# Cosine attention and a highway layer on one core: the gate's bias moved to VectorE, the norm of k moved into the exponential

## The chip, the core and the metric

The kernel runs on one core of a Trainium2 chip. A time is the device time of one execution in microseconds; the median of the runs shown counts. The core's engines work side by side and each takes its own instructions strictly in the order of the program: TensorE (PE; its weight loads are shown apart as PEld), VectorE (DVE), ScalarE (ACT), GpSimd (POOL) and SyncE (SP), which here only starts transfers. An instruction that waits holds up everything behind it on its engine.

## What is computed

```python
def _attn_ref(q, k, v, tau):                    # (8, 12, 448, 64): batch, heads, rows, depth
    q_n = q / (np.linalg.norm(q, axis=-1, keepdims=True) + 1e-06)
    k_n = k / (np.linalg.norm(k, axis=-1, keepdims=True) + 1e-06)
    scores = np.matmul(q_n, k_n.transpose(0, 1, 3, 2)) / tau
    scores = scores - np.max(scores, axis=-1, keepdims=True)
    attn = np.exp(scores)
    attn = attn / (np.sum(attn, axis=-1, keepdims=True) + 1e-09)
    return np.matmul(attn, v).astype(np.float32)

def _moe_ref(x, w_h, w_t, b_t):                 # x is (3584, 768), the weights (768, 768)
    H = np.maximum(x @ w_h, 0.0)
    T = 1.0 / (1.0 + np.exp(-(x @ w_t + b_t)))
    return (T * H + (1.0 - T) * x).astype(np.float32)
```

The attention's 12 heads of 64 columns side by side are the 768 columns of x. The scores are cosines over tau = 0.1, so they are bounded and the kernels leave the row maximum out. T is the gate and b_t its bias.

## The kernel before

The work goes by batch (8 of them), and in a batch by pairs of heads (6), 48 steps s in all. Of the 448 rows, 384 lie as three chunks on 128 partitions each (qr, kr, vr); the last 64 of two heads share the partitions of one more tile (qt, kt, vt).

For each batch the squares of q and k are summed (sq, f, n) and turned into 1/norm in rs: by a logarithm and an exponential on ScalarE for batch 0, by seven Newton steps on VectorE for the others (`steps`, lines 447 to 472). `scaled` (525) multiplies q and k of a pair by it into qn, on GpSimd or VectorE; `ktnorm` and `qtnorm` do the same for the last rows into kb. qn is then turned (queries and keys on the free side) into qT: by TensorE, with a copy out of PSUM, for batches 0 to 3, by a transposing transfer on SP for the others.

`scores` (621) is the heart. For each of three chunks of 128 keys TensorE writes the scores of both heads of a pair, 128 keys by 2 x 448 queries, into one of three pairs of PSUM banks (S, named pS), and ScalarE takes the exponential of all 896 columns in one instruction (line 643) into E, with the factor 1/tau as a constant. The last 64 keys of both heads go through a bank of the other ring of two (B, named pB) and one exponential of 512 columns (656) into Et. `attend` then multiplies E with v; a column of ones in vp gives the row sum, whose reciprocal (713) scales the result into x (715).

`ffn` (731) makes the highway layer for a batch in four groups of rows, three of 128 x 768 and one of 128 x 384. The gate's products with wt and those with wh each fill one of the three S slots; the gate's sum begins with two products of a tile of ones with the bias (bth, lines 777 and 793), which put the bias into PSUM. ScalarE takes the tanh out of PSUM (816, 817) into tt, VectorE forms max(H, 0) - x out of PSUM (830), maps tt to the gate (835), multiplies (838), and VectorE or GpSimd adds x (844) into os, from which SP stores. os is a ring of four buffers.

The order of all of this is written out by hand: `ORDER` lists the numbered operations, `SLOTS` the buffer that each takes from its ring, `MOVED` those that go to their second choice of engine. Operations of VectorE and GpSimd that are marked `port` also keep the order of the list between them. The highway layer of a batch is spread over the attention of the next. The few lines that matter are these:

```python
def fe(c=c):                                                             # line 642
    return nc.scalar.activation(R("E", s)[:, c, :, 0:448], R("S", 3 * s + c)[:, :, 0:448], AF.Exp, scale=inv_tau)
...
lt, rh = (ones[ln, 0:128], bth[ln, cols]) if cc < 0 else (xT[ln, cc, :], w_[ln, cc, cols])
```

Of the kernel before, what the change touches and what calls it, by code (L numbers as in the profile page):

```python
# [12 lines left out]
ALU = mybir.AluOpType  # L13
# [83 lines left out]
1121010122010000100121121000010222112011102100120012100102110110211012100011012310120002210110001102010110220100  # L97
1010020122111020211001100201010111200101200000000102111210001210022102001201002011102110110020112011112001020220
0001102102110100110021102212100210001220001010200122110012110211101013200000021102101220110002122102101102100010
20121001001011100201321000122201012223  # L100
""".replace("\n", "")
)

# [862 lines left out]
```

## Time and profile before

| | |
|---|---|
| median of 3 runs | 272.5 us (270.1, 272.5, 274.83) |
| span of the profiled execution, first to last instruction | 268.0 us |
| mean granted clock of TensorE | 0.967 |
| moved by the transfer engines | 43.14 MB, mean 161 GB/s |

The profile covers one execution from its first to its last instruction. The time of a run is taken outside and holds a little more than the span; the profiled execution's own time isn't listed apart, so its span stands beside the runs: 4.5 us under their median, 2.1 us under the lowest. A row that groups instructions gives line, engine, operation, output and inputs, shape and count, then the group's busy time and the mean duration of one in ns, then how long the engine had been idle before them and what ended it. A row of the timeline gives start, duration from the first start to the last end, and the same names. A row by stretches gives its bounds, its length, the busy time of the engines named in the text with the number of instructions, then TensorE's granted clock, the share of the transfer engines and GB/s.

### The profile page before, as it was taken

To read this page: it belongs to the slowest core of one execution; us is meant where nothing else is said; L and a number is where in the kernel's file an instruction comes from. 1 tells how busy PE (TensorE), PEld (TensorE's weight loads), DVE (VectorE), ACT (ScalarE), POOL (GpSimd) and SP (SyncE) were. 2 spreads that over 40 slices of the span, in tenths; PEclk is the share of its full clock that TensorE was granted. 3 is DMA by queue.
4 is the path that set the end of the run, shared out by engine and by line. 5 is a ranking of instruction groups with operands and counts; after the bars stand their busy time and mean duration, and the time that the engine had idled before them with its cause. 6 is when DMAs were issued, how large, how long until landed. Compare 5 with 4: busy or idle time off the path is not lost.

```text
span 268.0 us, 9080 instructions
## 1 busy us (share of the span) xinstructions
PE 243.8 (91%) x3783; PEld 164.3 (61%) x3783; DVE 220.0 (82%) x501; ACT 206.1 (77%) x279; POOL 116.2 (43%) x150
## 2 busy tenths in 40 slices
PE   6088987899999999999999998999999999999990
PEld 2043665667776667666766775766567757777650
DVE  6598999999999989997999988999877953556483
ACT  3378999789999989989788898969778897671210
POOL 8757359455554567335551535226132501141200
PEclk9567999999999999999999999999999999999996
DMA  7999999999969696999889999999757837123143
GB/s 131 210 192 183 178 199 210 196 183 193 149 97 224 145 172 65 192 213 199 206 136 155 186 244 162 193 137 224 173 115 214 134 63 177 59 92 120 32 181 101
DMA packets 103738, 43.14 MB, mean 161 GB/s; under 512 B 97552, under 2 KB 100624, under 8 KB 103696
## 3 DMA queue, kind: packets, MB, share of 16 engines
q0 software_dynamic: 38464, 16.32, 49.1%
q1 hardware_dynamic: 64000, 25.80, 47.4%
q8 instruction: 30, 0.49, 0.7%
q10 hardware_dynamic: 1232, 0.43, 0.7%
q14 instruction: 12, 0.10, 0.1%
HBM read 37.82 MB, written 11.01 MB: 182 GB/s over the span
## 4 chain that ended last, share of the span: by engine, by line
PE 64%; DVE 17%; DMA 8%; issue 4%; ACT 2%; POOL 2%; SPq 1%; DVEq 0%; POOLq 0%; ACTq 0%
PE pS L793 27%; PE pS L637 8%; PE pB L689 7%; PE pS L777 6%; DMA qT<-qn 6%; PE pB L652 4%; PE pB L705 3%; PE pB L685 3%; PE pB L577 3%; DMA qr<-in_q_dram 2%; DVE os L844 2%; DVE x L715 2%; DVE f L416 2%; PE pB L306 1%; DVE kb L254 1%
## 5 line engine op out<-in xcount | busy, mean ns | idle before, releaser
L643 ACT ACTIVATE E<-pS 128x896 f16<-128x896 f32 x144 | 127.4, 924 | 23.1 <-PE pS L637 21.9
L793 PEld LDWEIGHTS <-xT 64*128 64x128 f16 x1152 | 54.5, 94 | 31.2 <-issue 1.3
L793 PE MATMUL pS<-wh,xT 64*128 64x384 f16 x576 | 58.0, 323 | 0.0
L793 PE MATMUL pS<-wt,xT 64*128 64x384 f16 x576 | 57.1, 323 | 0.0
L637 PE MATMUL pS<-qT 64*128 64x384 f16 x288 | 43.5, 331 | 1.8 <-DMA qT<-qn 1.0
L689 PE MATMUL pB<-vp,E 128*128 128x65 f16 x864 | 43.3, 194 | 0.0
L830 DVE SCALAR_TENSOR_TENSOR hm<-pS,x 128x768 f16<-128x768 f32 (+1 forms) x33 | 27.3, 834 | 17.5 <-PE pS L793 6.9
L689 PEld LDWEIGHTS <-E 128*128 128x128 f16 x864 | 38.5, 98 | 0.7 <-issue 0.6
L637 PEld LDWEIGHTS <-qT 64*128 64x128 f16 x576 | 22.7, 95 | 19.5 <-issue 4.6
L254 POOL TENSOR_TENSOR qn<-kr,rs 128x384 f16<-128x384 f16 x24 | 19.8, 828 | 32.5 <-issue 10.0
L685 PE MATMUL pB<-vp,Et 128*128 128x130 f16 x144 | 31.9, 222 | 0.5 <-DVE vp L257 0.4
L844 POOL TENSOR_TENSOR os<-x,hm 128x768 f32<-128x768 f16 (+1 forms) x11 | 16.7, 1516 | 34.6 <-DVE hm L838 16.4
L817 ACT ACTIVATE tt<-pS 128x768 f16<-128x768 f32 x24 | 19.6, 821 | 14.4 <-PE pS L793 14.3
L715 DVE SCALAR_TENSOR_TENSOR x<-pB,rd 128x448 f16<-128x448 f32 x48 | 29.8, 622 | 1.1
L656 ACT ACTIVATE Et<-pB 128x512 f16<-128x512 f32 x48 | 29.1, 610 | 1.7 <-PE pB L652 1.5
L637 PE MATMUL pS<-tT,qT 64*128 64x64 f16 x282 | 27.6, 190 | 0.0
L705 PE MATMUL pB<-vp,E 128*128 128x65 f16 x288 | 18.4, 194 | 0.6 <-DVE x L715 0.6
L254 POOL TENSOR_TENSOR qn<-qr,rs 128x384 f16<-128x384 f16 x17 | 14.4, 853 | 9.0 <-DVE os L844 3.5
L844 DVE TENSOR_TENSOR os<-x,hm 128x768 f32<-128x768 f16 (+1 forms) x21 | 17.6, 836 | 0.2
L685 PEld LDWEIGHTS <-Et 128*128 128x128 f16 x144 | 14.0, 97 | 5.6 <-issue 4.1
L254 DVE TENSOR_TENSOR qn<-qr,rs 128x384 f16<-128x384 f16 x30 | 16.8, 566 | 0.5 <-POOL qn L254 0.4
L713 DVE RECIPROCAL rd<-pB 128x7 f32<-128x7 f32 x48 | 9.4, 199 | 8.4 <-PE pB L705 4.0
(110 smaller groups left out, 437.4 us busy)
## 6 DMA issues: line engine op xcount, KB each, us to landing
out_dram<-os SPq DMA_DIRECT2D x24, 384.0 KB, 3.2
vr<-in_v_dram POOLq DMA_DIRECT2D x8, 576.0 KB, 11.7
kr<-in_k_dram POOLq DMA_DIRECT2D x7, 576.0 KB, 9.9
qr<-in_q_dram POOLq DMA_DIRECT2D x7, 576.0 KB, 10.2
qt<-in_q_dram SPq DMA_DIRECT2D x16, 96.0 KB, 5.2
vt<-in_v_dram SPq DMA_DIRECT2D x16, 96.0 KB, 5.2
out_dram<-os SPq DMA_DIRECT2D x16, 96.0 KB, 2.3
kt<-in_k_dram SPq DMA_DIRECT2D x14, 96.0 KB, 6.0
```

The lines of the kernel that those rows point to most:

```text
L254: return (nc.vector if eng == "DVE" else nc.gpsimd).tensor_mul(out_, a, c)
L637: ins = nc.tensor.matmul(dst, lhsT=qT[ln, 384 + 128 * c : 512 + 128 * c], rhs=rhs, start=True, stop=True)
L643: return nc.scalar.activation(R("E", s)[:, c, :, 0:448], R("S", 3 * s + c)[:, :, 0:448], AF.Exp, scale=inv_tau)
L656: op("ACT", f"expt {s}", lambda: nc.scalar.activation(R("Et", s)[:, 64:576], R("B", ("S", s))[:, :], AF.Exp, scale=inv_tau), key + 3, r=[( ...
L685: nc.tensor.matmul(U[:, 2 * c : 2 * c + 2, :].rearrange("p g e -> p (g e)"), lhsT=Et[:, 128 + 128 * c : 256 + 128 * c], rhs=vp[:, 6:8, :]. ...
L689: ins = nc.tensor.matmul(U[:, 2 * c + ab, :], lhsT=EF[:, j, 576 * ab + 128 * c : 576 * ab + 128 * c + 128], rhs=vp[:, 3 * ab + j, :], star ...
L705: ins = nc.tensor.matmul(U[:, 6, :], lhsT=lt, rhs=rh, start=(n == 0), stop=(n == 7))
L715: op("DVE", f"ev {s}", lambda: nc.vector.scalar_tensor_tensor(out=R("x", b)[:, :, D * p : D * p + D], in0=U_()[:, :, 0:D], scalar=0.0, in1 ...
L793: ins = nc.tensor.matmul(P[:, h, 0:MH], lhsT=lt, rhs=rh, start=(part == 0 and cc == (-1 if wi == 0 else 0)), stop=(part == 1 and cc == CC ...
L817: return nc.scalar.activation(T.rearrange("p (h m) -> p h m", h=2), P[:, :, 0:MH], AF.Tanh, scale=0.5)
L830: return nc.vector.scalar_tensor_tensor(out=o_, in0=i0, scalar=0.0, in1=xs, op0=ALU.max, op1=ALU.subtract)
L844: op(en, f"out{wd} {g}", lambda: eng.tensor_add(R("os", g)[:, 0:W], xall(), R("hm", g)[:, 0:W]), at + 0.1, r=[("gg", g), ("x", b)], w=[("o ...
```

## The change

Six edits, and with them the whole order is new.

- The gate's bias is no longer put into PSUM by products. It is spread over all partitions by its load (bth, and bt2 for the narrow group), and VectorE adds it while it reads the gate's products out of PSUM, into a buffer of os (called z here); the tanh reads z instead of PSUM. This holds for all batches (`ADDED`).
- k is no longer scaled: `carried` copies it into qn, on VectorE, GpSimd or ScalarE, and `ktnorm` copies too. Its 1/norm is applied in the exponential, as a scale that is read for each partition (a key) from rs. The two heads of a pair have different norms, so the exponential of 896 columns becomes two of 448; that of the last keys stays one. tau is taken into rs. This holds for all pairs (`RAW`) but the first. rs has four buffers instead of three.
- Each weight comes in two loads instead of one, and the first products wait for the half that they use.
- More operations may go to either of two or three engines (`ENGINES` in place of `MOVED`).
- The first pair of q and k is loaded into a buffer of os.
- A second load of ScalarE's function table is written out (before, one stood ahead of the first tanh).

```diff
+    RAW = tuple(range(8))
+    ADDED = tuple(range(8))
...
-    NR = dict(..., rs=3, qn=2,
+    NR = dict(..., rs=4, qn=2,
...
-        for w_src, w_dst, nm in ((moe_w_t, wt, "wt"), (moe_w_h, wh, "wh")):
-            op("POOL", f"ld {nm}", lambda w_src=w_src, w_dst=w_dst: nc.gpsimd.dma_start(
-                w_dst[:, :, :], w_src.rearrange("(cc p) m -> p cc m", p=128)), key, w=[(nm, 0)])
-        for n in range(2):
-            op("POOL", f"ld b {n}", lambda n=n: nc.gpsimd.dma_start(bth[64 * n : 64 * n + 1, :], moe_b_t), key,
-               w=[("bth", 0)], r=[("zb", 0)])
+        op("POOL", "ld b", lambda: nc.gpsimd.dma_start(bth[:, :], moe_b_t.partition_broadcast(128)), key, w=[("bth", 0)])
...
+        for hf in range(2):
+            for w_src, w_dst, nm in ((moe_w_t, wt, "wt"), (moe_w_h, wh, "wh")):
+                op("POOL", f"ldw {nm} {hf}", lambda w_src=w_src, w_dst=w_dst, hf=hf: nc.gpsimd.dma_start(
+                    w_dst[:, 3 * hf : 3 * hf + 3, :], w_src.rearrange("(cc p) m -> p cc m", p=128)[:, 3 * hf : 3 * hf + 3]), key,
+                   w=[(nm, hf)])
...
+    def carried(t, b, p, key):
+        s = 6 * b + p
+        eng = pick("DVE", "POOL", "ACT")
+        op(eng, f"kc {s}", lambda: copied(
+            eng, R("qn", s // 2)[:, s % 2, t].rearrange("l c ab d -> l ab c d"),
+            rows(t, b, p, p + 1)[:, :, 0, :].rearrange("l ab (c d) -> l ab c d", c=NCH)), key,
+           r=[rowtok(t, b, p)], w=[("qn", s // 2, s % 2)], port=True)
...
             def fe(c=c):
+                if raw(b, p):
+                    at = col(b, p) + 6 + c
+                    for ab in range(2):
+                        ins = nc.scalar.activation(R("E", s)[:, c, ab, 0:448], R("S", 3 * s + c)[:, ab, 0:448], AF.Exp,
+                                                   scale=R("rs", b)[:, 0, at + NCH * ab : at + NCH * ab + 1])
+                    return ins
                 return nc.scalar.activation(R("E", s)[:, c, :, 0:448], R("S", 3 * s + c)[:, :, 0:448], AF.Exp, scale=inv_tau)
...
-            R("Et", s)[:, 64:576], R("B", ("S", s))[:, :], AF.Exp, scale=inv_tau), key + 3,
+            R("Et", s)[:, 64:576], R("B", ("S", s))[:, :], AF.Exp,
+            scale=R("rs", b)[:, 0, 6 + p : 7 + p] if raw(b, p) else inv_tau), key + 3,
...
-                for cc in range(lo - (1 if wi == 0 and lo == part == 0 else 0), hi):
+                for cc in range(lo - (1 if biased and lo == part == 0 else 0), hi):
...
+                if added:
+                    def biased_gate():
+                        P, Z = R(*bank_of(g, 0, tail)), R("os", ("z", g))
+                        if tail:
+                            return nc.vector.tensor_add(Z[:, 0:MH], P[:, 0, 0:MH], bt2[:, :])
+                        return nc.vector.tensor_add(Z.rearrange("p (h m) -> p h m", h=2), P[:, :, 0:MH],
+                                                    bth.rearrange("p (h m) -> p h m", h=2))
+
+                    op("DVE", f"bz{1 if tail else 2} {g}", biased_gate, at, r=[("Pd", g, 0), ("bt2" if tail else "bth", 0)],
+                       w=[("z", g)], u=[bank, ("os", ("z", g))])
+
...
+                    if added:
+                        return nc.scalar.activation(T[:, 0:W], R("os", ("z", g))[:, 0:W], AF.Tanh, scale=0.5)
```

Of the new tables, two lines stand for all:

```diff
-18 17 2 3 5 0 77 20 19 33 82 21 6 23 11 4 83 24 29 22 76 1 16 8 73 86 28 74 41 25 36 80 40 9 42 27 26 35 32 43
+18 20 24 28 5 29 11 30 0 21 19 22 25 1 26 27 33 32 31 34 23 37 283 36 35 58 121 281 4 10 6 17 9 15 7 13 8 46 47 96
```

What the new order makes of it is seen in the built programs. On ScalarE, well into the second half, exponentials of E and Et stand between tanhs (tt); before, an exponential of a chunk is one instruction of 2 x 448 columns:

```order
L643 ACTIVATE E_107<-pS_132 128x2x448
L656 ACTIVATE Et_111<-pB_134 128x512
L643 ACTIVATE E_107<-pS_132 128x2x448
L643 ACTIVATE E_109<-pS_131 128x2x448
L257 COPY vp_87<-vr_81 128x6x64
L817 ACTIVATE tt_120<-pS_130 128x768
```

and in the changed kernel, at a like place:

```order
L671 ACTIVATE E_109<-pS_131,rs_99 128x448 x2
L688 ACTIVATE Et_111<-pB_135,rs_99 128x512
L671 ACTIVATE E_108<-pS_131,rs_99 128x448 x2
L863 ACTIVATE tt_123<-os_129 128x768
L671 ACTIVATE E_110<-pS_132,rs_99 128x448 x2
L671 ACTIVATE E_109<-pS_131,rs_99 128x448 x2
```

Each exponential of a chunk is now two instructions that read rs, and the tanh reads a buffer of os.

On VectorE, near the end, the highway layer's steps stand between the attention's reciprocals (rd) and scalings (x). Before:

```order
L830 TENSOR_SCALAR hm_125<-pS_131,x_115 128x768
L835 TENSOR_SCALAR tt_121<-tt_121 128x768
L715 TENSOR_SCALAR x_116<-pB_133,rd_113 128x7x64
L830 TENSOR_SCALAR hm_123<-pS_131,x_115 128x768
L715 TENSOR_SCALAR x_116<-pB_134,rd_114 128x7x64
L838 TENSOR_TENSOR hm_125<-tt_121,hm_125 128x768
```

Now:

```order
L854 TENSOR_TENSOR os_130<-pS_133,bth 128x768
L880 TENSOR_SCALAR hm_124<-pS_132,x_116 128x768
L880 TENSOR_SCALAR hm_126<-pS_131,x_116 128x768
L854 TENSOR_TENSOR os_129<-pS_133,bth 128x768
L885 TENSOR_SCALAR tt_123<-tt_123 128x768
L746 RECIPROCAL rd_114<-pB_135 128x7
L885 TENSOR_SCALAR tt_122<-tt_122 128x768
L748 TENSOR_SCALAR x_117<-pB_135,rd_114 128x7x64
```

The bias sums (os out of pS and bth) are new there, each ahead of the tanh whose result is mapped two or three rows on.

On VectorE, at the start, the first pair's norms (first_n) and products (qn out of first and first_rs) stand before among the squares and folds (sq, f) of the pairs that come after:

```order
L497 TENSOR_REDUCE first_n<-first_fb 128x15
L254 TENSOR_TENSOR sq_88<-kr_72 128x2x2x192
L501 TENSOR_TENSOR qn_100<-first,first_rs 128x2x3x64 x2
L511 TENSOR_TENSOR first_kb<-first_t,first_rs 64x64
L254 TENSOR_TENSOR sq_88<-kt_77 128x384
L416 TENSOR_TENSOR f_91<-sq_88 128x1152
L506 TENSOR_TENSOR first_qtn<-first_t,first_rs 128x128
```

Now:

```order
L509 TENSOR_REDUCE first_n<-first_fb 128x15
L523 TENSOR_TENSOR first_kb<-first_t,first_rs 64x64
L513 TENSOR_TENSOR qn_101<-os_127,first_rs 128x2x3x64 x2
L518 TENSOR_TENSOR first_qtn<-first_t,first_rs 128x128
L523 TENSOR_TENSOR first_kb<-first_t,first_rs 64x64
L259 COPY qT_105<-pB_135 128x896
L426 TENSOR_TENSOR f_91<-sq_88 128x1152
```

The first pair's products and the copy of its turned tile now come first, the folds of the next pairs behind them.

Counted over both programs: TensorE loses 64 bias products; VectorE gains 32 bias sums and loses 23 products of k, for which 16 copies come; 14 products of q go from VectorE to GpSimd, and GpSimd's 24 products of k become 24 copies; ScalarE has 282 exponentials of 448 columns in place of 141 of 896, 47 of its 48 exponentials of Et read rs, and 7 copies of k are new on it. Each kernel has six tanhs behind its last exponential.

More of the change, by code (lines that the diff above doesn't have):

```diff
@@ L247, with pick @@
     op = pl.op
-    def pick(one, other):
-        return other if len(pl.ops) in MOVED else one
+    def pick(*engs):
+        n = len(pl.choices)
+        pl.choices.append((len(pl.ops), engs))
+        return engs[ENGINES[n]]
     def product(eng, out_, a, c):
@@ L271, in clear @@
         for n, t in enumerate(tiles):
-            eng = pick("DVE", "POOL") if name in ("zE", "zEt", "zvp", "zkb") else "DVE"
+            eng = pick("DVE", "POOL")
             e = nc.vector if eng == "DVE" else nc.gpsimd
@@ L295 @@
     clear("zEt", TILES["Et"], lambda t: [(t[:, 0:64], 0.0), (t[:, 576:640], 0.0)], 3.1, 4)
[L296 removed]
+    clear("zb", [0], lambda t: [(ones[:, :], 0.0), (ones[:1, :], 1.0), (ones[64:65, 0:128], 1.0)], 20)
     fills = [0]
@@ L387, in rowtok, with square @@
         return ("qr" if t == 0 else "kr", b, p)
-    def square(b, p0, p1, key, engs=("DVE", "DVE"), tails=False):
+    def square(b, p0, p1, key, tails=False):
         g0 = 12 if tails else 0
@@ L393, in square @@
         i = (b, p0)
-        for t, eng in enumerate(engs):
-            eng = pick(eng, "DVE" if eng == "ACT" else "POOL" if b == 1 else "ACT")
+        for t in range(2):
+            eng = pick("DVE", "ACT", "POOL")
             def fn(t=t, eng=eng):
@@ L402, in square @@
             op(eng, f"sq{p1 - p0} {b} {p0} {t}", fn, key,
-               r=[rowtok(t, b, p) for p in range(p0, p1)] + [("tab", 0)], w=[("sq", i)], port=eng != "ACT")
+               r=[rowtok(t, b, p) for p in range(p0, p1)] + [("tab", 0)], w=[("sq", i)], port=True)
         if tails:
@@ L523, in rcol, with scaled @@
         return R("rs", b)[:, 0, c : c + 6].rearrange("l (ab c) -> l ab c", ab=2)
-    def scaled(t, b, p, key, eng):
+    def scaled(t, b, p, key):
         s = 6 * b + p
-        eng = pick(eng, "DVE")
+        eng = pick("POOL", "DVE")
         def fn():
@@ L767, in ffn, with tails_mm @@
             bank = bank_of(g, wi, tail)
-            def tails_mm(wi, w_, lo, hi):
+            added = wi == 0 and b in ADDED
+            biased = wi == 0 and not added
+            def tails_mm(wi, w_, lo, hi, biased=biased):
                 P, xT = R(*bank_of(g, wi, True)), xTg()
-                for cc in range(lo - (1 if wi == 0 and lo == 0 else 0), hi):
+                for cc in range(lo - (1 if biased and lo == 0 else 0), hi):
                     for h in range(2):
@@ L817, in tanh @@
                     return nc.scalar.activation(T.rearrange("p (h m) -> p h m", h=2), P[:, :, 0:MH], AF.Tanh, scale=0.5)
-                op("ACT", f"th{1 if tail else 2} {g}", tanh, at, r=[("Pd", g, 0)], w=[("tt", g)], u=[bank])
+                op("ACT", f"th{1 if tail else 2} {g}", tanh, at, r=[("z", g) if added else ("Pd", g, 0), ("tab2", 0)], w=[("tt", g)],
+                   u=[("os", ("z", g)) if added else bank])
             else:
@@ L830, in hmx @@
                         return nc.vector.scalar_tensor_tensor(out=o_, in0=i0, scalar=0.0, in1=xs, op0=ALU.max, op1=ALU.subtract)
-                    op("DVE", f"hm{2 // halves if not tail else 1} {g} {h}", hmx, at, r=[("Pd", g, 1), ("x", b)],
+                    op("DVE", f"hm{2 // halves if not tail else 1} {g} {h}", hmx, at, r=[("Pd", g, 1), ("x", b)] + ([("tt", g)] if tail and b not in ADDED else []),
                        w=[("hm", g)], u=[bank])
@@ L840, in ffn @@
            r=[("gt", g), ("hm", g)], w=[("gg", g)], u=[("tt", g), ("hm", g)], port=True)
-        last = b == B - 1 and i >= 2
-        en = "DVE" if last else pick("POOL", "DVE")
+        en = pick("POOL", "DVE")
         eng = nc.vector if en == "DVE" else nc.gpsimd
@@ L873 @@
             first_pair(3)
-            square(b, 1, 3, 6, ("ACT", "ACT"), True)
+            square(b, 1, 3, 6, True)
             newton(b, (6, 1, 2), 7)
-            square(b, 3, 6, 10, ("ACT", "ACT"))
+            square(b, 3, 6, 10)
             newton(b, (3, 4, 5), 11)
```

150 lines of the change are left out of this document (87 added, 63 removed), and 138 rows, old and new, of tables (MOVED, ORDER).

## The prediction

> **What bounds the kernel now.** I read the page's busy shares and its chain of waits first, then busy time by stretches, then ScalarE's instructions in order of time.
>
> ```profile
> PE 243.8 (91%) x3783; PEld 164.3 (61%) x3783; DVE 220.0 (82%) x501; ACT 206.1 (77%) x279; POOL 116.2 (43%) x150
> PE 64%; DVE 17%; DMA 8%; issue 4%; ACT 2%; POOL 2%; SPq 1%; DVEq 0%; POOLq 0%; ACTq 0%
> ```
>
> TensorE carries the end; ScalarE has only 2% of the chain. A share over the whole span says little here, so here are five stretches.
>
> ```profile
> 18.00:241.10 223.10, 215.50 (x3481) 147.50 (x3478) 191.64 (x429) 194.36 (x262) 99.14 (x123) 0.99 1.04 166
> 20.00:120.00 100.00, 95.12 (x1519) 65.51 (x1521) 93.79 (x215) 93.06 (x126) 54.89 (x70) 0.98 1.22 172
> 60.00:80.00 20.00, 19.87 (x350) 14.43 (x345) 18.86 (x38) 19.94 (x26) 11.08 (x13) 1.00 1.04 147
> 200.00:240.00 40.00, 40.00 (x666) 28.01 (x662) 23.95 (x50) 31.93 (x43) 11.49 (x13) 1.00 0.53 122
> 241.10:268.00 26.90, 19.89 (x271) 12.59 (x267) 15.37 (x31) 4.10 (x6) 2.90 (x2) 0.92 0.32 109
> ```
>
> After the comma stand PE, weight loads, DVE, ACT and POOL. From 18.0 to 241.1 us the exponentials run, and the 26.9 us behind them are the last products. In the exponential stretch ScalarE is busy 194.4 of 223.1 us: 93% over the first 100 us, 19.94 of 20 at its fullest, 80% near the end. It is nearly as full as TensorE and hides in the chain because it is just fast enough. It has 223.1 - 194.4 = 28.7 us to give.
>
> **The exponentials.** These rows price them:
>
> ```profile
> L643 ACT ACTIVATE E<-pS 128x896 f16<-128x896 f32 x144 | 127.4, 924 | 23.1 <-PE pS L637 21.9 <-PE pB L689 0.4
> L656 ACT ACTIVATE Et<-pB 128x512 f16<-128x512 f32 x48 | 29.1, 610 | 1.7 <-PE pB L652 1.5
> 18.02 1.73 ACT L643 ACTIVATE E<-pS 128x896 f16<-128x896 f32 x2 [0.65 <-PE pS L637]
> 91.85 0.64 ACT L656 ACTIVATE Et<-pB 128x512 f16<-128x512 f32 x1
> 92.33 0.97 ACT L643 ACTIVATE E<-pS 128x896 f16<-128x896 f32 x1
> 159.73 4.16 ACT L643 ACTIVATE E<-pS 128x896 f16<-128x896 f32 x5
> 240.16 0.92 ACT L643 ACTIVATE E<-pS 128x896 f16<-128x896 f32 x1
> ```
>
> An exponential over 896 columns lasts 0.924 us, but five in a row take 4.16 us, so the next one begins after (4.16 - 0.92) / 4 = 0.81 us. One over 512 columns gives way after 92.33 - 91.85 = 0.48 us. The line through both is 0.86 ns a column, so 448 columns hold the engine for 0.48 - 64 x 0.00086 = 0.43 us. The scale of a score now differs from row to row and between the two heads of a pair, so 141 of the 144 exponentials become two of 448 columns whose scale is read from rs. Halving alone costs 2 x 0.43 - 0.81 = 0.05 us each, 7 us in all. The scale from memory is the larger question; the nearest rows are the logarithm, which reads its bias from a tile, and the exponential behind it, which reads none.
>
> ```profile
> L449 ACT ACTIVATE rs<-n,tiny 128x36 f32<-128x36 f32 x2 | 0.7, 338 | 0.8 <-DVE n L422 0.8
> L451 ACT ACTIVATE rs<-rs 128x36 f32<-128x36 f32 x2 | 0.5, 243 | 0.0
> 20.41 0.35 ACT L449 ACTIVATE rs<-n,tiny 128x36 f32<-128x36 f32 x1
> 20.64 0.93 ACT L643 ACTIVATE E<-pS 128x896 f16<-128x896 f32 x1
> ```
>
> At equal shape the operand costs 338 - 243 = 95 ns. The logarithm of 20.41 overlapped its follower by 0.35 - 0.23 = 0.12 us, as the wide exponentials do (0.924 - 0.81 = 0.11), so the 95 ns are engine time and not hidden. A half then holds ScalarE 0.43 + 0.095 = 0.525 us, a pair 1.05 us, 0.24 us more than now: 141 x 0.24 = 34 us. The 47 exponentials over 512 columns that read rs add 47 x 0.095 = 4.5 us. Lower bound: operand free, 7 us for the halves. Upper: the second half of a pair also loses its overlap with the first, 141 x 0.11 = 15 us more. I take 34 + 4.5, since the same operand was seen at work on the same engine.
>
> By the Trainium skill (ScalarE: Activation LUTs, What ACT_TABLE_LOAD costs) each pointer operand adds about 93 ns to 186 + 0.833 N, and neighbours overlap by about 93 ns. The trace agrees on the operand (95) and differs on the overlap (110 to 120); by the page a pair would hold the engine 1.12 us, and the exponentials would cost some 10 us more than in my sum, which goes by the rows.
>
> **The rest of ScalarE.** By the programs it loses one large square, four small ones and three copies of 896 columns, and gains some 17 copies of 384 to 768 columns (seven of k, three each of kt and vt, three of xT, one of tT) against two fewer of vr. At the row below less the overlap, 0.4 us each, I put the balance at +2 us.
>
> ```profile
> L257 ACT COPY vp<-vr 128x384 f16<-128x384 f16 x10 | 5.1, 527 | 0.0
> ```
>
> ScalarE in the exponential stretch: 194.4 now. A break after an exponential shows as a longer share (127.4 / 144 = 0.885 against 0.81), and a full engine has none, so back to back it is 194.4 - 144 x 0.075 = 183.6. After: 183.6 + 34 + 4.5 + 2 = 224, 235 if the breaks stay, and 239 if the halves don't overlap. The stretch had 223.1. At the 93% of the fullest 100 us it becomes 224 / 0.93 = 241 us. The slack near the end goes too. Here is the stretch from 200 to 240 us for E alone and for Et alone (busy, count):
>
> ```profile
> 200.00:240.00 40.00, 23.40 (x27) 1.00 0.53 122
> 200.00:240.00 40.00, 5.96 (x10) 1.00 0.53 122
> ```
>
> They would add 27 x 0.24 + 10 x 0.095 = 7.4 us to 31.93 busy of 40, so that stretch is 98% full. What is late next is TensorE at the scores: a score bank is held 1.05 us instead of 0.81, and the programs give both the same three.
>
> **Gate bias.** Rows of the products that leave and of the sums that come:
>
> ```profile
> L793 PE MATMUL pS<-bth,ones 64*128 64x384 f16 x48 | 8.0, 325 | 0.2 <-ACT tt L816 0.2
> L777 PE MATMUL pS<-bth,ones 128*64 128x384 f16 x16 | 2.8, 347 | 0.0
> 95.16 0.34 PE L793 MATMUL pS<-bth,ones 64*128 64x384 f16 x2 [0.23 <-ACT tt L816]
> 95.32 1.15 PE L793 MATMUL pS<-wt,xT 64*128 64x384 f16 x12
> L830 DVE SCALAR_TENSOR_TENSOR hm<-pS,x 128x768 f16<-128x768 f32 x23 | 21.9, 955 | 13.4 <-PE pS L793 6.9 <-ACT E L643 4.4 <-POOL os L844 1.8
> L830 DVE SCALAR_TENSOR_TENSOR hm<-pS,x 128x384 f16<-128x384 f32 x10 | 5.5, 554 | 4.1 <-ACT E L643 2.0 <-PE pS L777 1.8 <-ACT tt L816 0.4
> ```
>
> Two bias products hold TensorE only 95.32 - 95.16 = 0.16 us; 32 pairs are 5 us, of which 5 pairs (0.8 us) lie behind the last exponential. The rest lies where ScalarE will set the pace and brings nothing. VectorE gets 24 sums of 768 columns and 8 of 384 out of PSUM. The nearest row by source and shape is hm: 24 x 0.955 + 8 x 0.554 = 27 us. Each stands between TensorE and the tanh, and the sum, not the tanh, now frees the bank. Behind a sum on VectorE are queued the reciprocals that free the attention's banks.
>
> **k and the moves.**
>
> ```profile
> L254 POOL TENSOR_TENSOR qn<-kr,rs 128x384 f16<-128x384 f16 x24 | 19.8, 828 | 32.5 <-issue 10.0 <-DVE tt L835 9.7 <-DVE rs L466 6.1
> L254 DVE TENSOR_TENSOR qn<-kr,rs 128x384 f16<-128x384 f16 x23 | 13.4, 596 | 0.1
> L257 POOL COPY vp<-vr 128x384 f16<-128x384 f16 x19 | 9.5, 507 | 13.1 <-DVE kb L254 4.6 <-DVE qn L254 2.7 <-DVE sq L254 1.6
> L257 DVE COPY vp<-vr 128x384 f16<-128x384 f16 x19 | 6.0, 323 | 0.0
> L254 DVE TENSOR_TENSOR qn<-qr,rs 128x384 f16<-128x384 f16 x30 | 16.8, 566 | 0.5 <-POOL qn L254 0.4
> L254 POOL TENSOR_TENSOR qn<-qr,rs 128x384 f16<-128x384 f16 x17 | 14.4, 853 | 9.0 <-DVE os L844 3.5 <-DVE qn L254 2.5 <-DMA qT<-qn 1.9
> L844 DVE TENSOR_TENSOR os<-x,hm 128x768 f32<-128x768 f16 x15 | 14.2, 948 | 0.1
> ```
>
> VectorE loses 23 products of k (13.7 us) for 16 copies (5.2), hands 14 products of q (7.9) and three wide output sums (2.8) to GpSimd. With the bias sums that is 27 - 13.7 + 5.2 - 7.9 - 2.8 = +8 us; with it VectorE is busy at most 191.64 + 8 = 200 of 241 us, so it is not the bound. GpSimd gains the 14 products of q (14 x 0.853 = 12 us) and saves 24 x (0.828 - 0.507) = 8 on k; it stays far from full at 99.14 of 223.
>
> **Weights and order at the start.**
>
> ```profile
> 8.28 0.22 ACT L451 ACTIVATE first_rs<-first_rs 128x15 f32<-128x15 f32 x1
> 12.78 0.76 DVE L416 TENSOR_TENSOR f<-sq 128x1152 f16<-128x1152 f16 x1 [0.99 <-ACT sq L260]
> 13.79 0.29 PE L613 MATMUL pB<-ident,first_qtn 128*128 128x128 f16 x1 [8.21 <-DVE first_qtn L506]
> wh<-in_moe_w_h_dram POOLq DMA_DIRECT2D x1, 1152.0 KB, 22.7
> wt<-in_moe_w_t_dram POOLq DMA_DIRECT2D x1, 1152.0 KB, 26.8
> ```
>
> The first pair's norms are ready at 8.5 us, yet TensorE gets its first turn at 13.8, since VectorE's order puts squares and folds of the next pairs, which wait for their loads, ahead of first_qtn. In the new order only the first pair's own products stand there, four at most at 0.57 us (the row of q): the turn comes at 10.8, 3 us earlier, and the first exponential, 4.2 us behind it now (18.02 - 13.79), at 15. ScalarE's order puts fewer squares and copies in between, so I take 14, and 18 as the other end. The weights' halves, each half of the 22.7 or 26.8 us, are wanted later: by the programs the first tanh stood behind 27 wide exponentials and stands behind 35. If a half is late, the queue of TensorE stops there, and a few us go.
>
> **The sum.** First exponential 14, stretch 241, behind it 26.9 - 0.8 = 26: a span of 281. The span before, 268.0, is 4.5 us under the median of the runs, 272.5 (2.1 under the lowest, 270.1); I add 4.5: 285.5 us. With 239 / 0.93 = 257 in place of 241 it is 301, and with the breaks of now and the first exponential still at 18, 18 + 235 / 0.93 + 26 + 4.5 = 301; with ScalarE never idle, 14 + 224 + 26 + 4.5 = 268.5.
>
> **The rivals.** *The scale is free* (0.10): a pointer fetched while the neighbour runs would leave 224 - 282 x 0.095 - 4.5 = 193 us, or 207 at 93%, less than TensorE needs. Then TensorE's 223.1 - 4 for the bias products holds, and the time is 14 + 219 + 26 + 4.5 = 264, faster (268 if the early start is lost). Against it: the logarithm's 0.23 us before its follower. For it: a bias, not a scale, of another function, three times in all. *Half is hidden* (0.08): (224 + 193) / 2 = 209, at 93% 225: 270 us, no change. *The gate sums become the wait* (0.08): tanh stands in ScalarE's order ahead of exponentials; where VectorE, 93.79% full over the first 100 us, comes to the sum late, everything behind it waits. It decides if most of the 26 sums before the last exponential arrive a sum's length (0.955 us) late: 25 us more, 311 us. That z takes its buffers from the four of os, which the stores also hold, works the same way. My forecast has the other 0.74, of which some 0.08 falls within 2%, where ScalarE is over 96% full.
>
> The runs of before spread over 270.1 to 274.8 us, so under about 2% (267 to 278) is no change. Faster: 0.09, nearly all of the first rival. Same: 0.08 + 0.08 = 0.16. Slower: 0.75. The range 268 to 301 leaves out the first and third rival.
>
> **What would show it.** ScalarE over 90% busy from the first to the last exponential, and busy 235 us or more in all; halves of 0.64 us, each 0.53 after the one before; TensorE waiting for ScalarE at the scores; first exponential near 14 us; the stretch behind the last one near 26. If halves follow each other within 0.45 us the price is wrong; if ScalarE idles before tanh for VectorE, the third rival is right.

## The result: 17 us slower, and the profile after

The changed kernel takes 289.8 us (median of 4 runs, 288.8 to 291.7) against 273.0 for before on the same chip (median of 4, 270.1 to 274.8): a ratio of 1.066, 95% interval 1.057 to 1.075. Runs more than 1.5% above the fastest of their kernel are left out of all ratios and, from here on, of medians and differences, as for before the run of 274.8 (272.5 without it, so 17.3 us). The profiled execution is the run of 291.67 us, with a span of 289.9.

The busy shares and the chain of waits of the changed kernel, as the page has them:

```profile
PE 250.4 (86%) x3719; PEld 167.7 (58%) x3719; DVE 223.3 (77%) x498; ACT 241.3 (83%) x429; POOL 135.6 (47%) x178
ACT 36%; PE 31%; DMA 6%; DVE 5%; issue 5%; SPq 0%; ACTq 0%; DVEq 0%
```

ScalarE's share of the chain rose from 2% to 36% and TensorE's fell from 64% to 31%. ScalarE's busy time rose by 35 us, from 206.1 to 241.3. The stretches below are what lies under these shares: from the first exponential to the last, four pieces of that, and what lies behind it (columns as before: bounds, length, PE, weight loads, DVE, ACT, POOL, clock, transfers, GB/s).

```profile
15.10:263.40 248.30, 226.38 (x3458) 153.89 (x3455) 196.26 (x438) 230.67 (x411) 116.25 (x150) 0.98 1.00 153
60.00:80.00 20.00, 18.67 (x300) 12.86 (x298) 17.90 (x40) 20.00 (x36) 14.11 (x19) 1.00 1.47 177
100.00:120.00 20.00, 14.99 (x198) 9.61 (x199) 13.35 (x28) 14.09 (x26) 7.24 (x12) 0.83 1.23 162
200.00:240.00 40.00, 38.27 (x623) 27.00 (x621) 29.32 (x67) 37.58 (x69) 16.01 (x24) 1.00 0.71 141
222.00:263.40 41.40, 39.84 (x663) 27.93 (x659) 26.55 (x56) 36.68 (x66) 11.47 (x17) 1.00 0.62 126
263.40:289.90 26.50, 18.43 (x239) 11.41 (x236) 17.55 (x33) 5.81 (x8) 5.65 (x4) 0.95 0.30 105
```

ScalarE is busy 230.7 of 248.3 us, 93%, and between 60 and 80 us it never stops, while TensorE now has gaps there. The slack near the end is smaller: 37.58 us of 200 to 240, 31.93 before. The stretch of before, though, ended just ahead of its last exponential; in the like stretch of the changed kernel, 222 to 263.4, ScalarE is busy 36.68 of 41.4 us, 89% against 80% before. One piece stands out the other way: from 100 to 120 us everything is short of work, ScalarE 14.09 of 20 and TensorE 14.99. The exponentials, grouped and in order of time (start, duration from first start to last end, names, count):

```profile
L671 ACT ACTIVATE E<-pS,rs 128x448 f16<-128x448 f32 x282 | 162.3, 695 | 14.3 <-PE pS L662 14.0
L688 ACT ACTIVATE Et<-pB,rs 128x512 f16<-128x512 f32 x47 | 35.4, 762 | 1.0 <-PE pB L684 0.8
24.56 4.28 ACT L671 ACTIVATE E<-pS,rs 128x448 f16<-128x448 f32 x8
28.70 0.56 ACT L262 ACTIVATE sq<-qt 128x384 f16<-128x384 f32 x1
47.18 5.36 ACT L671 ACTIVATE E<-pS,rs 128x448 f16<-128x448 f32 x10
```

Eight halves begin at 24.56 and the square behind them at 28.70, so a half holds the engine (28.70 - 24.56) / 8 = 0.52 us, near the 0.525 of the forecast. A half lasts 0.695 us on average, where 0.64 was forecast; some 0.17 us of it run under the instruction behind it, another half or not. So 162.3 / 282 = 0.576 us is more than a half's share of the engine: in that sum the last half of each row of halves counts to its end. Taken from its start to the start of the next instruction, or to its own end where ScalarE then stands idle, a half takes 0.53 us on average over the 282.

TensorE now waits for ScalarE at the scores. The row of the changed kernel and that of before (total, times, longest, us):

```profile
PE pS L662 <- ACT E L671: 5.2, 16, 0.7
PE pS L637 <- ACT E L643: 0.5, 2, 0.3
```

### The profile page after: what moved, and what is told of

Its sections match the earlier page's. It is cut to its first block, busy times and chain, and to the rows that moved or that the text cites. A ratio compares the mean times of both kernels' runs of the same rounds, so it can differ in the third digit from the quotient of the medians.

```text
span 289.9 us, 9118 instructions
## 1 busy us (share of the span) xinstructions
PE 250.4 (86%) x3719; PEld 167.7 (58%) x3719; DVE 223.3 (77%) x498; ACT 241.3 (83%) x429; POOL 135.6 (47%) x178
## 4 chain that ended last, share of the span: by engine, by line
ACT 36%; PE 31%; DMA 6%; DVE 5%; issue 5%; SPq 0%; ACTq 0%; DVEq 0%
ACT E L671 25%; PE pS L829 15%; ACT Et L688 4%; PE pS L662 4%; ACT sq L262 4%; DMA xT<-x 3%; PE pS L813 3%; PE pB L722 3%; ACT tt L863 3%; DMA kt<-in_k_dram 2%; PE pB L738 1%; PE pB L718 1%; PE pB L600 1%; PE pB L684 1%; DVE hm L880 1%
## 5 line engine op out<-in xcount | busy, mean ns | idle before, releaser
L671 ACT ACTIVATE E<-pS,rs 128x448 f16<-128x448 f32 x282 | 162.3, 695 | 14.3 <-PE pS L662 14.0
L662 PE MATMUL pS<-qT 64*128 64x384 f16 x288 | 46.6, 336 | 7.7 <-ACT E L671 5.2
L893 POOL TENSOR_TENSOR os<-x,hm 128x768 f32<-128x768 f16 (+1 forms) x17 | 24.2, 1428 | 42.2 <-DMA out_dram<-os 13.6
L256 POOL TENSOR_TENSOR qn<-qr,rs 128x384 f16<-128x384 f16 x31 | 26.0, 845 | 25.3 <-DVE tt L885 14.6
L863 ACT ACTIVATE tt<-os 128x768 f16<-128x768 f32 (+1 forms) x32 | 26.0, 820 | 12.6 <-DVE os L854 11.1
L688 ACT ACTIVATE Et<-pB,rs 128x512 f16<-128x512 f32 x47 | 35.4, 762 | 1.0 <-PE pB L684 0.8
L854 DVE TENSOR_TENSOR os<-pS,bth 128x768 f32<-128x768 f32 x24 | 22.7, 953 | 6.2 <-PE pS L829 4.7
L259 POOL COPY qn<-kr 128x384 f16<-128x384 f16 x24 | 13.0, 540 | 21.6 <-DVE hm L888 9.3
L600 PE MATMUL pB<-ident,qn 128*128 128x128 f16 x144 | 13.2, 231 | 9.6 <-DVE qn L513 7.6
L259 POOL COPY vp<-vr 128x384 f16<-128x384 f16 x20 | 11.2, 568 | 19.5 <-DVE f L430 8.6
```

What stands on the lines that cost most here:

```text
L256: return (nc.vector if eng == "DVE" else nc.gpsimd).tensor_mul(out_, a, c)
L259: return nc.scalar.copy(out_, a) if eng == "ACT" else (nc.vector if eng == "DVE" else nc.gpsimd).tensor_copy(out_, a)
L662: ins = nc.tensor.matmul(dst, lhsT=qT[ln, 384 + 128 * c : 512 + 128 * c], rhs=rhs, start=True, stop=True)
L671: ins = nc.scalar.activation(R("E", s)[:, c, ab, 0:448], R("S", 3 * s + c)[:, ab, 0:448], AF.Exp, scale=R("rs", b)[:, 0, at + NCH * ab : a ...
L688: op("ACT", f"expt {s}", lambda: nc.scalar.activation(R("Et", s)[:, 64:576], R("B", ("S", s))[:, :], AF.Exp, scale=R("rs", b)[:, 0, 6 + p ...
L863: return nc.scalar.activation(T[:, 0:W], R("os", ("z", g))[:, 0:W], AF.Tanh, scale=0.5)
```

## The experiments

The experiments ran in four batches, each on one chip with runs of before beside it. The medians of before, counted as above, were 270.8 (kernels b_halves_ptr, b_halves, b_full_ptr, b_gate), 271.5 (a_full_imm, a_halves_imm, a_scaled, b_start), 271.5 (a_gate_pe, a_gate_pe_imm, b_gate_late) and 271.0 us (a_xt_early). Differences are to those; ratios, with 95% intervals, are of the same runs and not quotients of these medians.

### The exponentials alone, in the order of before

Three kernels keep the program of before and change only the exponentials. First, two halves of 448 columns whose scale is read from a small tile sc that holds 1/tau in every row (results unchanged):

```diff
-return nc.scalar.activation(E[:, c, :, 0:448], S[:, :, 0:448], AF.Exp, scale=inv_tau)
+for ab in range(2):
+    ins = nc.scalar.activation(E[:, c, ab, 0:448], S[:, ab, 0:448], AF.Exp, scale=sc[:, :])
+return ins
```

> The kernel before, with one thing added: every exponential but the first pair's reads its scale (1/tau) from a tile, and those of 896 columns are two of 448. Theory (ScalarE's price is the cause): 183.6 + 34 + 4.5 = 222 us of ScalarE in the exponential stretch, at 93% 239 us in place of 223: 16 us more, 283 to 294. Rival (the gate sums on VectorE and the waits of the new order are the cause): under 278.

Second, the halves with the constant scale:

```diff
-    ins = nc.scalar.activation(E[:, c, ab, 0:448], S[:, ab, 0:448], AF.Exp, scale=sc[:, :])
+    ins = nc.scalar.activation(E[:, c, ab, 0:448], S[:, ab, 0:448], AF.Exp, scale=inv_tau)
```

> The kernel before with halves of 448 columns and a constant scale. Theory: 7 us more of ScalarE, 191 us, at 93% 205, which is less than TensorE's stretch of 223: 0 to 4 us more, 272 to 277. Rival (halving itself, with twice the instructions and a bank held longer, is the price, not the operand): 283 or more.

Third, whole exponentials that read the scale from sc:

```diff
-return nc.scalar.activation(E[:, c, :, 0:448], S[:, :, 0:448], AF.Exp, scale=inv_tau)
+return nc.scalar.activation(E[:, c, :, 0:448], S[:, :, 0:448], AF.Exp, scale=sc[:, :])
```

> The kernel before with whole exponentials that read their scale from a tile. Theory: 141 x 0.095 + 4.5 = 18 us more of ScalarE, 202 us, at 93% 217, still under 223, but the fullest 100 us have no room: 2 to 9 us more, 275 to 282. Rival (the operand is hidden behind the neighbour): no change, 271 to 275.

Measured: 289.6 us (18.8 more; ratio 1.072, 1.066 to 1.078) for both together, 272.0 (1.2 more; 1.006, 1.001 to 1.011) for the halves, 276.5 (5.7 more; 1.024, 1.017 to 1.031) for the operand. All three lie where the theory of ScalarE's demand put them. The groups of the three kernels, and a run of exponentials from each. Halves and operand:

```profile
L646 ACT ACTIVATE E<-pS,sc 128x448 f16<-128x448 f32 x282 | 160.5, 686 | 12.1 <-PE pS L638 11.5
35.48 5.37 ACT L646 ACTIVATE E<-pS,sc 128x448 f16<-128x448 f32 x10
```

Halves with the constant:

```profile
L645 ACT ACTIVATE E<-pS 128x448 f16<-128x448 f32 x282 | 134.5, 578 | 18.2 <-PE pS L637 17.2 <-PE pB L693 0.5
34.12 4.47 ACT L645 ACTIVATE E<-pS 128x448 f16<-128x448 f32 x10
```

Whole, with the operand:

```profile
L644 ACT ACTIVATE E<-pS,sc 128x896 f16<-128x896 f32 x141 | 137.5, 1029 | 15.6 <-PE pS L638 15.1 <-PE pB L690 0.3
35.13 4.61 ACT L644 ACTIVATE E<-pS,sc 128x896 f16<-128x896 f32 x5
```

Ten halves back to back take 5.37 us with the operand and 4.47 without: 0.09 us for each instruction, engine time and not hidden. Five whole ones take 4.61 against 4.16 before: 0.09 again. So the price is by instruction, and halving doubles how often it is paid. The three also show how slack works. By the forecast's own prices the halves, the operand and both ask ScalarE for 7, 18 and 38.5 us more (its busy time on the three pages rises by 6.9, 13.8 and 34.1 from 206.1); the time rises by 1.2, 5.7 and 18.8 us. The engine had 28.7 us idle in the exponential stretch: here a demand well below that was nearly free, and one in the middle cost a third. That this is because the idle time isn't where the demand falls fits the stretches of before (19.94 us busy of 20 at the fullest, 80% near the end), but wasn't tested by itself.

### The gate's sums alone, in the order of before

The program of before, without the bias products; VectorE adds the bias while it copies the gate's products from PSUM into tt, just ahead of each tanh.

```diff
-return nc.scalar.activation(T, P, AF.Tanh, scale=0.5)
+nc.vector.tensor_add(T, P, bth)
+return nc.scalar.activation(T, T, AF.Tanh, scale=0.5)
```

> The kernel before with the gate edit alone: 32 bias sums on VectorE out of PSUM, each ahead of its tanh, no bias products on TensorE. Theory (ScalarE's price is the cause of the 17 us): TensorE gives 5 us, VectorE gets 27 where its fullest 100 us have 6 to spare; a small loss, 270 to 279. Rival (the gate sums are the cause): 283 or more.

Measured: 288.7 us, ratio 1.069 (1.062 to 1.075). This is 17.9 us more: the theory's expectation missed, and the rival's number came. The chain of b_gate, what ScalarE waited for (total, times, longest), and the stretch from 40 to 220 us:

```profile
DVE 30%; PE 29%; issue 8%; ACT 6%; POOL 1%; DVEq 0%; ACTq 0%; POOLq 0%
ACT tt L828 <- DVE tt L826: 35.1, 23, 5.4
40.00:220.00 180.00, 163.93 (x2617) 113.95 (x2616) 171.31 (x373) 148.56 (x200) 79.37 (x96) 1.00 1.07 165
```

The wait at the tanh in before, where TensorE ended it, and the same stretch of before and of the changed kernel, in this order:

```profile
ACT tt L817 <- PE pS L793: 14.3, 7, 5.4
40.00:220.00 180.00, 175.15 (x2852) 120.05 (x2851) 162.40 (x364) 158.10 (x214) 83.22 (x100) 1.00 1.06 170
```

```profile
40.00:220.00 180.00, 164.53 (x2539) 112.29 (x2537) 146.22 (x333) 170.32 (x302) 92.03 (x113) 0.98 1.04 154
```

VectorE is the third number with a count: 162.4 of 180 us before, 171.3 with the sums alone, 146.2 in the changed kernel. At 95% it is the fullest engine of b_gate, and the tanh, which stands ahead of exponentials, makes ScalarE wait for it 23 times. Is it the place of the tanh or VectorE's work? The next kernel puts each sum directly behind its last product and each tanh up to 30 places later:

```diff
-products of the gate | (2 to 31 places) | sum, tanh
+products of the gate, sum | (up to 30 places more, ahead of gt) | tanh
```

> Before with the gate's bias added by VectorE, as in b_gate (16 us slower), but each sum stands directly behind its last product in the order and each tanh up to 30 places later, ahead of the operation that reads it, as far as the order leaves room. If the 16 us were the in-order ScalarE waiting at the tanh for VectorE (35 us of waits): 273 to 281 us, with those waits below 15 us. Rival, VectorE's work itself (27 us more on an engine 94% full over the first 100 us): 285 to 290 us wherever the tanh stands.

Measured: 294.9 us, 23.4 more, ratio 1.085 (1.076 to 1.093): above both ranges. The waits at the tanh did fall, and came back elsewhere (at the scores 13.1 us in b_gate):

```profile
ACT E L725 <- PE pS L719: 34.3, 38, 2.8
ACT tt L906 <- DVE tt L889: 17.8, 6, 6.0
```

So this later tanh is no remedy. The rival, VectorE's work, is the nearer, but the kernel lies 5 us above its range too, and the sums moved with the tanhs, so what the extra time over b_gate is stays open. That VectorE has no room for the sums in the order of before, and that the other edits make that room in the changed kernel, fits the three stretches above; no run takes the room away from the changed kernel, so it is argued, not shown.

### The changed kernel without the operand, and with k scaled again

Both kernels leave the norm of k out of the scores: one with whole exponentials, one with halves, both with a constant scale; all else is the changed kernel.

```diff
-scale=R("rs", b)[:, 0, at + NCH * ab : at + NCH * ab + 1]
+scale=1.0
```

> The changed kernel with one exponential of 896 columns and a constant scale in place of the two halves that read rs, for all pairs, and a constant scale for Et; the norm of k is left out. Theory (ScalarE's price is the cause): ScalarE's 230.7 us in the stretch lose 34 + 4.5 and become 192, under what TensorE needs; the time falls to 262 to 274. Rival (gate sums and the new order's waits): stays above 283.

> The changed kernel with its halves, but with a constant scale for them and for Et; the norm of k is left out. Theory (the operand is engine time): 282 x 0.095 + 4.5 = 31 us less, 230.7 becomes 199, at 93% 214, about TensorE's need: 264 to 277. Rival (the operand is hidden): above 285.

Measured: 277.6 us (6.2 more; 1.020, 1.010 to 1.030) and 278.6 (7.1 more; 1.026, 1.020 to 1.031), some us above the ranges of the theory and well below its rival. Reading the scale is therefore worth 6.6% - 2.6% = 4.0% of the time of before, some 11 us of the 17, and halving nothing that can be told once the scale is a constant. Some 6 to 7 us remain that are not the exponentials'. A page row of a_halves_imm, a stretch and its first half, and the two waits of TensorE in it that matter here:

```profile
PE 245.0 (88%) x3719; PEld 163.0 (59%) x3719; DVE 223.5 (81%) x498; ACT 216.0 (78%) x429; POOL 135.8 (49%) x178
80.00:120.00 40.00, 32.97 (x464) 20.90 (x461) 32.84 (x73) 31.53 (x60) 18.89 (x24) 0.96 1.01 142
80.00:100.00 20.00, 15.60 (x206) 9.59 (x202) 19.79 (x41) 16.90 (x31) 11.30 (x13) 1.00 1.16 149
PE pS L828 <- DMA xT<-x: 3.9, 1, 3.9
PE pS L662 <- DVE os L853: 1.0, 1, 1.0
```

The same 40 us of before:

```profile
80.00:120.00 40.00, 39.76 (x618) 26.80 (x616) 37.81 (x89) 37.19 (x53) 20.54 (x22) 1.00 1.14 165
```

TensorE works 32.97 us of these 40, before 39.76: 6.8 us are lost here, about as much as remains. It isn't one cause: 3.9 us are a wait for one transfer of x into xT, the rest is waits for VectorE (1.0 us for a sum of the gate, 1.0 for a scaling x, 0.9 for hm); VectorE is busy 19.79 of the first 20 us.

The next kernel scales k by products again, on VectorE and GpSimd, with one exponential of 896 columns and a constant scale as in before; products that stood ahead of their norms in the new order were moved behind them.

```diff
-copied(eng, qn[:, s % 2, t], rows(k, b, p))
+product(eng, qn[:, s % 2, t], rows(k, b, p), rs(b, p))
```

> The changed kernel with k scaled by products again (on VectorE and GpSimd, those that came before their norms moved behind them in the order) and whole exponentials with a constant scale; gate sums, weights in four loads and the rest of the order stay. Theory: ScalarE about 188 us in the stretch, no longer the bound; VectorE gets some 15 us of products back and has 196 + 15 = 211 of a stretch of 223 or less: 266 to 280. Rival: above 283.

Measured: 300.0 us, 28.6 more, ratio 1.108 (1.098 to 1.117), a miss. What ScalarE waited for, in a_scaled:

```profile
ACT E L754 <- PE pS L742: 41.2, 37, 5.0
ACT tt L943 <- DVE os L934: 16.6, 7, 5.0
```

ScalarE idles for want of scores. A product must stand behind its norm where a copy need not, and here the products stand ahead of other work of VectorE and GpSimd; that this is what holds the scores up is argued. TensorE's granted clock was also lower, 0.92 to 0.93 in the four runs against 0.966 to 0.981 in those of before, and what part of the 28.6 us goes with that isn't separated. This shows that the new order doesn't suit scaled k; what the scaling would cost in an order of its own it does not show.

### The rest: start, gate and a late transfer

Before, with the first pair's own products, turns and scores moved ahead of the squares and folds of later pairs (VectorE's order, in words):

```diff
-first_rs | squares and folds of the next pairs | first pair's last products
+first_rs | first pair's products | squares and folds of the next pairs
```

> The kernel before with the first pair's products, turn and scores moved ahead of the squares and folds of the next pairs. If the start is on the path, the first exponential comes 2 to 4 us earlier and the time falls by 1 to 4 us: 268 to 272. Rival (the loads of the next pairs set the pace there anyway): no change.

Measured: 271.6 us, ratio 1.002 (0.995 to 1.009): no change, as the rival has it. ScalarE's first rows in b_start:

```profile
12.62 1.73 ACT L717 ACTIVATE E<-pS 128x896 f16<-128x896 f32 x2
...
19.66 0.91 ACT L331 COPY qT<-pB 128x896 f16<-128x896 f16 x1 [2.74 <-PE pB L654]
```

And the copy of the next pair's qT in before:

```profile
19.63 0.91 ACT L257 COPY qT<-pB 128x896 f16<-128x896 f16 x1
```

The first exponential comes 5.4 us earlier than the 18.02 of before, and the next pair at the same time as there. ScalarE does squares of later pairs and then idles 2.74 us, so the early start is worth nothing in this kernel.

The changed kernel with the tanh taken straight from PSUM again, by ScalarE, at the place where VectorE's sum stood, once with the operand and once with a constant scale:

```diff
-op("DVE", f"bz{...} {g}", lambda: nc.vector.tensor_add(Z, P, bth), ...)
+op("ACT", f"bz{...} {g}", lambda: nc.scalar.activation(T, P, AF.Tanh, scale=0.5), ...)
 ...
-op("ACT", f"th{...} {g}", lambda: nc.scalar.activation(T, Z, AF.Tanh, scale=0.5), ...)
```

> The changed kernel, but the gate's bias enters PSUM by products again, and ScalarE takes the tanh straight from PSUM at the place in the order where VectorE's sum stood; all else, the scale read from rs included, stays. If ScalarE's demand from first to last exponential sets the time and the sums cost little in the new order: 283 to 290 us (the two tanh waits of 5 us in the last stretch go, some of it is given back to 5 us of bias products on TensorE). Rival, the sums cost here what they cost in the order of before (16 us): 272 to 278 us.

> As a_gate_pe, and the halves read a constant scale, so that the norm of k is left out of the scores. Of the changed kernel's 17 us some 11.5 went with the operand; this asks where the rest is. If it is the gate's sums on the way from TensorE to the tanh: 269 to 275 us. If it is the rest of the new order (late transposing transfers, loads, the start): 276 to 283 us, within 2 us of the same kernel with the sums.

As built, the bias products were not issued (TensorE has 3719 products, as in the changed kernel), so both leave the gate's bias out; the second leaves out the norm of k too. Measured: 296.9 us (25.4 more; 1.092, 1.084 to 1.100) and 283.0 (11.5 more; 1.041, 1.026 to 1.056; two runs, 281.0 and 285.0). The first is slower by 2.6% or some 7 us than the changed kernel, though less is computed, and misses both of its ranges. The second is some 4 us above a_halves_imm, with intervals that overlap, so it decides nothing. What VectorE and ScalarE waited for in a_gate_pe:

```profile
DVE rd L746 <- PE pB L722: 25.5, 20, 3.4
ACT tt L854 <- PE pS L829: 12.0, 5, 5.0
PE pS L662 <- ACT tt L854: 5.8, 5, 3.2
```

Here the tanh frees the bank of the products, and TensorE waits 5.8 us for it at the scores, which it never does for a tanh in the changed kernel; ScalarE waits 12.0 us at the tanh for TensorE, about as long as for the sums in the changed kernel (11.1). The reading, argued from these rows: a tanh that frees the bank must stand early, whereas with the sums the tanh can wait its turn. So the sums are better in this order than tanhs in their place; whether they are a part of the remaining 6 to 7 us these two kernels don't show.

Last, the stall between 80 and 120 us, as it stands in the changed kernel's chain and timeline:

```profile
99.64 9.49 DMA xT<-x
109.17 1.14 PE L829 MATMUL pS<-wt,xT 64*128 64x384 f16 x6 [3.85 <-DMA xT<-x]
110.73 2.21 ACT L671 ACTIVATE E<-pS,rs 128x448 f16<-128x448 f32 x4 [3.92 <-PE pS L662]
```

The edit of the order, in words, SyncE's first and then TensorE's:

```diff
-load qt | transpose x into xT
+transpose x into xT | load qt
-gate's products 0 | scores, scores | products 1 | turn | products 2 | scores | products 3 | turn, av
+scores, scores | turn | scores | turn, av | gate's products 0, 1, 2, 3
```

> The changed kernel, with one stall of its new order attacked: in the trace the transposing transfer of x that begins at 99.64 us (9.49 us long) is started only after a load of qt that waits for VectorE, and TensorE then waits 3.85 us for it with the scores of three chunks queued behind, so that ScalarE stands 3.92 us ahead of 110.73. Here the transfer stands ahead of that load, and the four product groups that need it stand behind those scores. If a full ScalarE gets back what it stood idle: 284.5 to 287.5 us, and the 20 us around it full. Rival, the products that now come later are waited for in their place (by VectorE's sum and the bank it frees): 288.5 to 291 us, no change.

Measured: 288.5 us, 17.5 more, ratio 1.064 (1.058 to 1.069): at the lower edge of the rival's range, no change that can be told from the 1.066 of the changed kernel. The exponentials where ScalarE stood, a tanh behind them and the stretch around them, in a_xt_early:

```profile
106.16 3.26 ACT L748 ACTIVATE E<-pS,rs 128x448 f16<-128x448 f32 x6
113.00 0.84 ACT L940 ACTIVATE tt<-os 128x768 f16<-128x768 f32 x1 [2.79 <-DVE os L931]
100.00:120.00 20.00, 16.03 (x241) 11.04 (x239) 14.98 (x34) 16.55 (x30) 8.21 (x10) 1.00 1.05 147
```

Six halves now run from 106.16 us on, where ScalarE stood; it is busy 16.55 of these 20 us instead of 14.09, 2.5 us more. But the rival's wait came as well: a tanh now waits 2.79 us for VectorE's sum of products that come later. So a part of the stall was moved, not removed. The same wait for a transfer stands in a_halves_imm (3.9 us, above); the edit was tried on the kernel that is bound by ScalarE, not on that one, so its share of the remainder isn't shown. No kernel tried is faster than before.

## Why the prediction was right, and which terms were off

**The mechanism** came as forecast: ScalarE is filled by the halves and by the scale read from memory, the operand is not hidden, and it sets the time at 93% busy. b_halves_ptr shows it with nothing else changed (18.8 us), a_halves_imm by taking the operand away (11 us). The rivals with a free or half-hidden scale fall by the same rows: 0.09 us an instruction, in three kernels.

**The sum** against the profiled execution: first exponential 15.1 us (14 forecast), stretch 248.3 (241), behind it 26.5 (26), what lies around the span 291.67 - 289.9 = 1.8 (4.5). The first three are 8.9 us over, the last 2.7 under, and this execution is 1.9 above its median: 285.5 + 8.9 - 2.7 - 1.9 = 289.8. That the sum came within 4.3 us is in part luck: the 4.5 us around the span was taken from medians and was too large, and hides 2.7 us of what the span lacked.

**The stretch** is the mis-sized term: ScalarE's demand was put at 224 us and is 230.7. The price of a half was right (0.525 us forecast, 0.52 measured). What failed is the step "a full engine has none", which took 144 x 0.075 = 10.8 us of breaks out of the 194.4 of before. Its 0.885 us an exponential is a sum in which the last of each row counts to its end, though the instruction behind it, an Et or a tanh, has often begun. Taken from its start to the start of the next instruction, or to its own end where ScalarE then stands idle, an exponential of before takes 0.837 us on average over the 144, so the breaks were 144 x (0.837 - 0.81) = 4 us and the step took out 7 too many, as much as the demand came out too low. And a part of them stayed: 0.53 us a half on average against 0.52 in a row is 3 us over 282. The other value in the text, 235 if the breaks stay, was the nearer. The 93% was right by its average, though not by its cause, and that is luck: part of the missing 7% is the one stall from 100 to 120 us, which the forecast of late weights or moved transfers didn't name.

**The first exponential.** The new order does bring the first pair first, but the rows of the changed kernel show what took back 1 to 2 us:

```profile
9.27 2.97 DVE L513 TENSOR_TENSOR qn<-os,first_rs 128x384 f16<-128x384 f32 x2
9.27 1.05 POOL L368 DMA_DIRECT2D vr<-in_v_dram  x1
10.34 1.48 POOL L256 TENSOR_TENSOR sq<-qr 128x768 f16<-128x768 f16 x1
12.30 0.82 PE L600 MATMUL pB<-ident,qn 128*128 128x128 f16 x6 [7.60 <-DVE qn L513]
15.08 0.60 ACT L688 ACTIVATE Et<-pB 128x512 f16<-128x512 f32 x1 [0.76 <-PE pB L684]
```

The two products of 1.02 us before take 2.97, and TensorE's first turn comes at 12.3, not 10.8. That an early start shortens the whole, as the sum has it, would need the engine behind it to stay full; b_start shows 5.4 us of it worth nothing in the kernel before. What it was worth in the changed kernel no run shows.

**Gate bias.** The duration was right (24 sums of 0.955 us forecast, 0.953 measured, next row), and so was VectorE not being the bound: 196.3 of 248.3 us.

```profile
L854 DVE TENSOR_TENSOR os<-pS,bth 128x768 f32<-128x768 f32 x24 | 22.7, 953 | 6.2 <-PE pS L829 4.7 <-ACT Et L688 1.3
ACT tt L863 <- DVE os L854: 11.1, 4, 5.0
```

The tanh waits for a wide sum 4 times, two of them (4.8 and 5.0 us) behind the last exponential. The third rival, the sums as the wait, didn't come here. What held it off is, it seems, the room on VectorE: the forecast took 19 us off it on k, q and the output sums, and in b_gate, where only the sums are made, without that cover, they cost 17.9 us. The prediction counted the cover; it didn't price its loss.

**What the parts add up to.** The exponentials alone cost 18.8 us and the sums alone 17.9, and all edits together 17. They don't add; the likely reason is that each was paid on another engine and the changed kernel relieves one of the two. Its 17 us are some 11 for the operand, shown, and 6 to 7 more. For these the trace of a_halves_imm points to the 40 us from 80 to 120, with one late transfer and a full VectorE; how they share it stays open.

## What to carry to other kernels

Before work is moved to an engine off the chain, set its demand against that engine's idle time in the stretch where it falls: with 28.7 us idle here, 7 more cost about 1 us, 18 a third of itself and 38.5 half. The scale read from memory was paid by instruction (0.09 us at 448 columns and at 896), so such an operand should go into few, wide ones; splitting an instruction to make the operand possible pays twice. And an edit that costs little in a new order can cost 18 us alone, where another edit may be its cover: price the cover when judging one of them.

## What the hardware showed that was not expected

- At the start, two products on VectorE took 2.97 us (row above) where before they took 1.02, the row below. GpSimd issued a load from 9.27 and ran squares from 10.34 to 11.82 us meanwhile, and VectorE's pair ended at 12.24, just behind the squares.

```profile
9.92 1.02 DVE L501 TENSOR_TENSOR qn<-first,first_rs 128x384 f16<-128x384 f32 x2
```

  In a_halves_imm, where the same squares run at the same time, the two products take 1.03 us and the product behind them is the long one (0.28 us in before):

```profile
10.14 2.29 DVE L518 TENSOR_TENSOR first_qtn<-first_t,first_rs 128x128 f16<-128x128 f32 x1
```

  The Trainium skill (SBUF — State Buffer, SBUF: two separate sides) says that a VectorE operation with two inputs from SBUF and a GpSimd operation that reads SBUF block each other, and that the one that starts first holds the port to its end. The rows agree with the blocking, in both kernels; they don't show the order, since by its record the product that waits begins ahead of the squares (9.75 and 10.14 against 10.34). No run here separates it from another cause.
- TensorE's granted clock fell to 0.83 in the stretch from 100 to 120 us of the changed kernel, where it was busy least of the stretches shown; in a_xt_early, with that wait shortened, it is 1.00 there.
- The time around the span was 1.8 us in the changed kernel's profiled run and 1.7 to 1.9 in the profiled runs of the experiments, not the 4.5 us that the forecast took from medians.
